# A one-core attention and feed-forward kernel: first loads reordered, first tile transposed in halves, a new TensorE order

## Chip, core and metric

The kernel runs on one core of a Trainium2 chip. The time is device microseconds of one execution; the metric is the median of several. The core has a matrix engine (TensorE, PE in the profile; PEld is its weight load), VectorE (DVE), ScalarE (ACT), GpSimd (POOL) and SyncE (SP). SyncE and ScalarE issue the loads, stores and DMA transposes here. Matmuls accumulate in PSUM, eight banks of 512 float32 columns in each of 128 partitions; everything else lies in SBUF.

## What is computed

A layer norm, then the sum of three things: x itself, a linear attention with softmax feature maps (16 heads of 28), and a feed-forward block with silu. Sizes: 2048 tokens, width 448, feed-forward width 1792, all bfloat16.

```python
def _A_ref(x, wqkv, w_phi, wo):
    qkv = (x @ wqkv).reshape(B, S, 3, H, Dh)  # then transposed: q, k, v per head
    pq = einsum("bhsd,hdf->bhsf", q, w_phi); pk = einsum("bhsd,hdf->bhsf", k, w_phi)
    phi_q = concatenate([softmax(pq), softmax(-pq)], -1)
    phi_k = concatenate([softmax(pk), softmax(-pk)], -1)
    kv = einsum("bhsf,bhsd->bhfd", phi_k, v);  z = einsum("bhsf->bhf", phi_k)
    o = einsum("bhqf,bhfd->bhqd", phi_q, kv) / (einsum("bhqf,bhf->bhq", phi_q, z) + 1e-6)
    return o.reshape(B, S, D) @ wo
def _B_ref(x, w1, w2):
    return silu(x @ w1) @ w2

xn = layernorm(A_x)
out = A_x + _A_ref(xn, A_wqkv, A_w_phi, A_wo) + _B_ref(xn, B_w1, B_w2)
```

## The kernel before

The kernel is a small list scheduler and a list of operations. Each operation names its engine, an assumed duration and what it reads and writes; the scheduler puts each engine's operations in an order and places semaphores. Most of TensorE's order is not left to it: `PLAN` is a list of words that was found by a search, and TensorE follows it strictly. A word `aF3@4` is the first half of feed-forward block 3 in banks 4 and 5, `bF3` its second half; `v`, `k`, `q` are projections of two tiles of 128 tokens; `f` folds w_phi into the q and k weights; `K` gathers kv, `U` is attention, `Y` and `F4:3` are parts of the second feed-forward product, `W`, `R`, `r`, `E` the product with wo and the output. The a, b and R words use 64 rows of the array in pairs, the others up to 128.

```python
PLAN = """aF3@4 aF4@0 bF3 aF5@2 av2@6 bF4 bv2 bF5 aF6@0 bF6 av0@4 bv0 aF7@0 aF8@2 aF10@4 bF8 bF10 bF7 f2@26 aF11@4 aF13@0 bF11
bF13 f0@26 aF9@4 aF12@0 bF9 av4@2 ak0@6 bv4 bF12 bk0 ...
... R3,6,13,1,5,10 F11@1:7 F11:6 F11:1 W11 r11"""
```

The loads, in the order of issue. Wp (w_phi) goes out on ScalarE's queue, the rest on SyncE's. `load_w1` loads the rows 0 to 383 of some columns of w1 and, as a second load, the last 128 rows.

```python
load(Wp[:], A_w_phi..., "wphi", eng="act", lat=3000.0)
load_x(0, 1)
load_x(1, 2)
load_x(2, 4)
load_w1(0, 512)
load_w1(512, 1024)
load_x(4, 8)
load_w1(1024, FF)
load_rows4(wv_sb, A_wqkv, 2 * D, 3 * D, "wv")
load_x(8, 12)
load_x(12, 16)
...   # w2 and wo, behind the transposes
```

Layer norm works on tiles of 128 tokens. Tiles 0 to 3 are turned over on TensorE into PSUM and copied to xnT; tiles 4 to 15 by DMA transposes of two tiles each.

```python
def ln_tile(t):
    ...  # bn_stats, bn_aggr (DVE), sqrt (ACT) and reciprocal (DVE) for t < 4, on POOL for the others
    if t < XN_DMA0:                                    # XN_DMA0 = 4
        norm(xn_sb[:, sl, 0:D], 0, D, 390)
    else:
        norm(xn_sb[:, sl, 0:KF], 0, KF, 370)
        norm(xn_sb[:, sl, KF:512], D - 128, D, 250)
    dstx = xnT[:, t, :, :]
    if t >= XN_DMA0:
        if t % 2:
            dma_t(xnT[:, t - 1:t + 1, ...], xn_sb[:, sl - 1:sl + 1, :], 1300.0, f"xnT_dma{t}", 1350.0)
        return
    tps = bank16[4 + t % 2][:, 0:512]...
    transposes([(tps[:, kt, :], xn_sb[:, sl, KS[kt]:KS[kt] + 128]) for kt in range(4)], f"tr{t}")
    if t < 3: act(dstx, tps, ACTF.Identity, 512, f"ev{t}")
    else:     copy(dstx, tps, 512, f"ev{t}")
```

The head of TensorE's work, ahead of the plan: feed-forward blocks 0, 1 and 2 (columns 0 to 255, 256 to 511, 512 to 767 of w1), token tile by token tile, since the tiles come one after another. For each tile and block there are six matmuls of 128 columns.

```python
head = [F(0, 0), F(1, 2), F(2, AUX)]
for t, fs in ((0, head[:2]), (1, head[:2]), (0, head[2:]), (1, head[2:]), (2, head), (3, head)):
    for f in fs:
        f[0](t * 128, t * 128 + 128)
for b, f in zip((0, 2, AUX), head):
    pe_mms(f[1](), "rest", ...)       # the last 64 rows, then
    f[3]()                            # silu on ScalarE
```

The transposes of SyncE have a fixed order. `wT_dma0` to `7` turn over columns of wqkv for the fold (they lie in the memory of Y_sb, where the profile shows them); the fold needs all eight.

```python
chain("wT_dma0 wT_dma1 wT_dma2 wT_dma3 xnT_dma5 wT_dma4 xnT_dma7 wT_dma5 wT_dma6 wT_dma7 xnT_dma9 xnT_dma11 ... w2 wo0 ...".split())
late = next(o.id for o in P.ops if o.name == "rstd15")    # GpSimd's ones come after it
```

At the end each engine's stream is written straight into the program:

```python
for ename, eng in (("sp", nc.sync), ("act", nc.scalar), ("pool", nc.gpsimd), ("dve", nc.vector), ("pe", nc.tensor)):
    emit_engine(ename, eng)
```

Of the kernel before, what the change touches and what calls it, by code (L numbers as in the profile page):

```python
# [140 lines left out]
class _Prog:  # L141
# [68 lines left out]
    def dma(self, fn, xfer, reads=(), writes=(), name="", out_slot=None, eng="sp", issue=480.0, lat=1700.0):  # L210
        o = self.op(eng, issue, fn, reads, writes, name=name)
        o.is_dma = True
        o.xfer = xfer
        o.lat = lat
        o.out_slot = out_slot
        return o

    def schedule(self):
        ops = self.ops
        n = len(ops)  # L220
# [19 lines left out]
        eng_free = {e: 800.0 if e == "sp" else 0.0 for e in ENGINES}  # L240
# [93 lines left out]
PLAN = """aF3@4 aF4@0 bF3 aF5@2 av2@6 bF4 bv2 bF5 aF6@0 bF6 av0@4 bv0 aF7@0 aF8@2 aF10@4 bF8 bF10 bF7 f2@26 aF11@4 aF13@0 bF11  # L334
bF13 f0@26 aF9@4 aF12@0 bF9 av4@2 ak0@6 bv4 bF12 bk0 av6@4 av8@2 ak4@0 bv8 bk4 bv6 av14@6 ak2@2 bv14 bk2 av12@0 ak6@4
bv12 bk6 ak8@6 av10@2 ak10@0 bv10 bk10 bk8 ak12@2 ak14@4 bk12 bk14 aq4@0 Y0@6:3 Y0:2 K0-6 bq4 aq6@4 K6-8 bq6 aq0@2 aq8@0
bq0 bq8 aF15@4 Y0:9 K8-12 bF15 aF19@2 aF14@0 bF19 bF14 aF17@5 s4 aF18@3 bF17 bF18 K12-16 aF16@5 aF21@2 aF24@0 bF21 bF16
bF24 M s6 aF27@2 aF26@4 bF27 aF22@0 bF26 bF22 aF20@6 aq2@2 bF20 aF23@0 aF25@4 bF23 bF25 bq2 U4 s8 F4@1:10 U9@0 s0 aq12@6
aq14@4 aq10@2 s2 bq12 bq10 bq14 F4:3 F4:1 F9@0:10 F8@3:3 F8:3 s10 W4 U8 s12 F8:6 Y1@4:14 F9:4 W9 U2 U0@5 F2@2:6 F2:8
F8:2 U7@6 U12@5 W8 Y3@4:9 Y3:5 W2 s14 W0@5 F7@4:9 F7:1 U1 F7:4 W7 R0,2 R8,7 R4,9 F10@6:5 U6@5 U10 F10:9 U3@3 F5@4:14  # L340
U13@2 F15@51:8 U15 F15:6 F12@2:5 F12:9 U14 F6@0:5 W12 E15 U5 F13@3:11 F6:9 F14@7:5 F13:2 F13:1 U11@1 W5 W3@5 r12 W13
F14:9 W14 r14 W6 W1@2 W10 R3,6,13,1,5,10 F11@1:7 F11:6 F11:1 W11 r11"""


def bass_parallel_sum__linear_kernel_hedgehog__dense_activation_silu__prompt_kernel(
# [12 lines left out]
    KP = 112  # L358
# [17 lines left out]
    with es:  # L376
# [148 lines left out]
        def load(dst, src, name, eng="sp", lat=1700.0):  # L525
            n = 2
            for _, cnt in list(dst.ap):
                n *= cnt
            P.dma(lambda e: e.dma_start(out=dst, in_=src), n / 280.0, writes=[dst], name=name, eng=eng, lat=lat)  # L529

        def load_x(t0, t1):
            load(x_sb[:, t0:t1, :], xt[:, t0:t1, :], f"x{t0}", lat=1400.0)

        def load_rows4(dst, src, c0, c1, name, lat=1700.0):
            load(dst[:, 0:3, :], src[0:KF, c0:c1].rearrange("(k p) f -> p k f", p=128), name, lat=lat)
            load(dst[:, 3, :], src[D - 128:D, c0:c1], name, lat=lat)

        def load_w1(c0, c1, lat=1700.0):
            load_rows4(w1_sb[:, :, c0:c1], B_w1, c0, c1, "w1", lat)

        load(Wp[:], A_w_phi.rearrange("(g hl) d f -> (hl d) g f", g=G), "wphi", eng="act", lat=3000.0)
# [3 lines left out]
        load_w1(0, 512)  # L545
        load_w1(512, 1024)
        load_x(4, 8)
        load_w1(1024, FF)
        load_rows4(wv_sb, A_wqkv, 2 * D, 3 * D, "wv")
        load_x(8, 12)  # L550
        load_x(12, 16)
        load(w2_sb[:], B_w2.rearrange("(f p) d -> p f d", p=128), "w2")
# [4 lines left out]
        def dma_t(dst, src, xfer, name, issue=1235.0, **kw):  # L557
            o = P.dma(lambda e: e.dma_start_transpose(out=dst, in_=src), xfer, lat=650.0, reads=[src] if kw.pop("sbuf", True) else [],
                      writes=[dst], name=name, issue=issue if xfer < 1500.0 else 2000.0, **kw)
            o.crowd = 1  # L560
# [10 lines left out]
        def fold_loads():  # L571
            for a in range(8):
                dma_t(wT_sb[:, a, :], A_wqkv[:, a * KP:a * KP + 128], 600.0, f"wT_dma{a}", (1600.0, 1400.0, 1780.0, 3280.0)[a] if a < 4 else 1300.0, sbuf=False)
# [22 lines left out]
        def ln_tile(t):  # L596
# [16 lines left out]
            def norm(dst, c0, c1, dur):  # L613
                P.op("dve", dur, lambda e: e.tensor_scalar(dst, x_sb[:, t, c0:c1], mv[:, t, 0:1], rstd[:, t:t + 1], ALU.subtract, ALU.mult),  # L614
                     reads=[xs, mv[:, t, 0:1], rstd[:, t:t + 1]], writes=[dst], name=f"xn{t}")

            if t < XN_DMA0:
                norm(xn_sb[:, sl, 0:D], 0, D, 390)
            else:
                norm(xn_sb[:, sl, 0:KF], 0, KF, 370)  # L620
                norm(xn_sb[:, sl, KF:512], D - 128, D, 250)
            dstx = xnT[:, t, :, :]
            if t >= XN_DMA0:
                if t % 2:
                    dma_t(xnT[:, t - 1:t + 1, :, :].rearrange("p i k c -> p (i k) c"),
                          xn_sb[:, sl - 1:sl + 1, :].rearrange("p i c -> p (i c)"), 1300.0, f"xnT_dma{t}", 1350.0)
                return
            tps = bank16[4 + t % 2][:, 0:512].rearrange("p (k c) -> p k c", k=4)
            transposes([(tps[:, kt, :], xn_sb[:, sl, KS[kt]:KS[kt] + 128]) for kt in range(4)], f"tr{t}")
            if t < 3:  # L630
                act(dstx, tps, ACTF.Identity, 512, f"ev{t}")
            else:
                copy(dstx, tps, 512, f"ev{t}")


# [3 lines left out]
        def pair_block(b0, width, lhs, rhs, name):  # L639
            def part(c0, c1):  # L640
                for i in range(2):
                    for n, kt in enumerate((0, 1, 2 + i)):
                        mm(banks[b0 + i][:, c0:c1], lhs(i, kt, slice(0, 128)), rhs(i, kt, slice(0, 128), c0, c1),
                           n == 0 and c0 == 0, False, name)
# [112 lines left out]
        def phi_q(t, pair=False):  # L757
# [8 lines left out]
            if n % 2 or not pair:  # L766
                n0, sp0 = (slot(t) - 1, sp - 1) if pair else (slot(t), sp)
                w = slot(t) - n0 + 1
                dma_t(phT[:, n0:n0 + w, :, :].rearrange("p t c j -> p (t c) j"), phq[:, sp0:sp0 + w, :, :].rearrange("p n c j -> p (n c j)"),
                      1300.0 * w, "phqT")  # L770
# [109 lines left out]
        chain("bnst0 bnag0 bnst1 bnag1 rstd0 xn0 rstd1 xn1 bnst2 bnag2 bnst3 bnag3 rstd2 xn2 rstd3 xn3 ev3".split())  # L880
        chain("ev0 ve2 ev1 ve3 ev2 silu_table".split())
        chain("tr0 tr1 tr2 tr3".split())
# [8 lines left out]
        for t, fs in ((0, head[:2]), (1, head[:2]), (0, head[2:]), (1, head[2:]), (2, head), (3, head)):  # L891
            for f in fs:
                f[0](t * 128, t * 128 + 128)
# [16 lines left out]
        chain("wT_dma0 wT_dma1 wT_dma2 wT_dma3 xnT_dma5 wT_dma4 xnT_dma7 wT_dma5 wT_dma6 wT_dma7 xnT_dma9 xnT_dma11 xnT_dma13 xnT_dma15 w2 "  # L910
              "wo0 wor0 wo1 wor1".split())
        memset(phq[:, :, :, KP:128], 0.0, 400, "phq0")
        late = next(o.id for o in P.ops if o.name == "rstd15")
        ones_column(0, NEK)
        ones_column(NEK, NT)
        for o in P.ops[-2:]:
            o.odeps.add(late)
# [138 lines left out]
        for ename, eng in (("sp", nc.sync), ("act", nc.scalar), ("pool", nc.gpsimd), ("dve", nc.vector), ("pe", nc.tensor)):  # L1056
            emit_engine(ename, eng)
# [28 lines left out]
```

## Time and profile before

| | |
|---|---|
| time, median of 3 | 150.25 us (150.01 to 151.19) |
| span of the profiled execution | 149.0 us |
| TensorE busy | 144.7 us |
| VectorE, ScalarE, GpSimd busy | 91.3, 70.2, 70.9 us |
| first matmul of the head | 6.96 us after the start |
| last sum begins | 146.64 us |

The profile is of one execution. Times are microseconds from the start of the span. A line of the time order has start, duration, engine, source line, operation, what it writes and reads with shapes and how many of them follow each other; in brackets how long the engine had been idle and what ended that. "L468" is the helper that issues all matmuls, so its rows are told apart by what they write and read: hT is the silu output, RA the normalised tile (its memory is later used by phi), phT at the start is w1. SPq and ACTq are the queues of SyncE and ScalarE. TensorE's end times are modelled, so its busy share says that there is a matmul in flight, not that it is at its peak.

### The profile page before, as it was taken

How to read it: one execution, taken by the hardware profiler on the slowest of the kernel's cores; microseconds unless marked ns; L12 is line 12 of the kernel's file. 1: busy time of each engine (PE TensorE's matmuls, PEld its weight loads, DVE VectorE, ACT ScalarE, POOL GpSimd, SP SyncE). 2: the span in 40 equal slices, each digit the busy share in tenths (PEclk: the TensorE clock that was granted, in tenths of full speed). 3: DMA queues.
4: the chain of work that ended last, by engine and by line, in shares of the span. 5: the costliest groups of instructions: out<-in, count | busy, mean ns of one | idle time of the engine just before them, and what ended most of it. 6: DMA issues, size and time to landing. Idle time of an engine off the chain costs nothing.

```text
span 149.0 us, 3394 instructions
## 1 busy us (share of the span) xinstructions
PE 144.7 (97%) x1412; PEld 79.9 (54%) x1412; DVE 91.3 (61%) x186; ACT 70.2 (47%) x86; POOL 70.9 (48%) x82
## 2 busy tenths in 40 slices
PE   7899999999999999999999999999999999999993
PEld 7694434555555565464544445455555567555541
DVE  1859898940198999211995027897552874243354
ACT  3567764557999997975475585910000000000000
POOL 7108568310049999999699900899600000000000
PEclk9999999999999999999999999999999999999999
DMA  5999975999400000000089494078966745240215
GB/s 101 334 372 336 178 134 106 191 243 344 108 0 4 0 4 4 0 4 0 0 94 191 86 186 79 6 139 160 127 139 134 187 116 106 37 101 5 68 68 179
DMA packets 44352, 17.41 MB, mean 117 GB/s; under 512 B 36784, under 2 KB 43952, under 8 KB 44336
## 3 DMA queue, kind: packets, MB, share of 16 engines
q1 hardware_dynamic: 41568, 15.36, 48.5%
q10 hardware_dynamic: 2768, 1.83, 3.8%
q8 instruction: 11, 0.18, 0.5%
q14 instruction: 5, 0.04, 0.1%
HBM read 6.56 MB, written 1.84 MB: 56 GB/s over the span
## 4 chain that ended last, share of the span: by engine, by line
PE 94%; DMA 3%; DVE 1%; SPq 1%; issue 0%; ACT 0%
PE psum L468 93%; DMA x_sb<-in_A_x_dram 3%; SPq L529 1%; DVE st L599 0%; DVE x_sb L842 0%; PE psum L483 0%; ACT ve L603 0%; DVE mv L600 0%
## 5 line engine op out<-in xcount | busy, mean ns | idle before, releaser
L468 PE MATMUL psum<-xnT,phT 64*128 64x512 bf16 (+1 forms) x428 | 45.1, 350 | 0.7 <-ACT ve L603 0.6
L468 PE MATMUL psum<-w_sb,hT 128*128 128x448 bf16 (+1 forms) x238 | 45.4, 342 | 0.0
L488 ACT ACTIVATE hT<-psum 128x1024 bf16<-128x1024 f32 x28 | 27.4, 1024 | 18.0 <-PE psum L468 18.0
L728 DVE TENSOR_REDUCE Rec<-Ek_sb 128x32 f32<-128x896 bf16 (+1 forms) x20 | 24.3, 1247 | 13.7 <-ACT Ek_sb L488 7.9
L468 PEld LDWEIGHTS psum<-xnT,phT 64*128 64x128 bf16 (+1 forms) x428 | 21.1, 95 | 21.3 <-ACT xnT L488 0.9
L468 PEld LDWEIGHTS psum<-w_sb,hT 128*128 128x128 bf16 x238 | 21.6, 98 | 19.0 <-issue 1.5
L763 POOL TENSOR_TENSOR RA<-Ek_sb,Rec 128x896 bf16<-128x896 bf16 x16 | 26.6, 1700 | 9.1 <-ACT Ek_sb L488 7.7
L468 PE MATMUL psum<-Wqk,xnT 64*128 64x432 bf16 x224 | 22.9, 343 | 0.0
L488 ACT ACTIVATE Ek_sb<-psum 128x864 bf16<-128x864 f32 x24 | 20.3, 932 | 2.9 <-issue 2.6
L738 POOL TENSOR_TENSOR Ek_sb<-Ek_sb,Rec 128x896 bf16<-128x896 bf16 x8 | 13.3, 1702 | 11.0 <-DVE Rec L729 11.0
L820 DVE TENSOR_SCALAR den<-psum 128x16 f32<-128x16 f32 x16 | 2.5, 161 | 22.3 <-PE psum L468 22.3
L468 PEld LDWEIGHTS psum<-Wqk,xnT 64*128 64x128 bf16 x224 | 10.6, 94 | 9.5 <-ACT Ek_sb L488 0.2
L738 POOL TENSOR_TENSOR phT<-phT,Rec 128x896 bf16<-128x896 bf16 x8 | 13.3, 1703 | 0.0
L468 PE MATMUL psum<-wv,xnT 64*128 64x448 bf16 x112 | 12.9, 349 | 0.1
L599 DVE BATCH_NORM_STATS2 st<-x_sb 128x6 f32<-128x448 bf16 x16 | 9.7, 605 | 4.2 <-DMA x_sb<-in_A_x_dram 4.1
L614 DVE TENSOR_SCALAR RA<-x_sb,mv,rstd 128x384 bf16<-128x384 bf16 (+2 forms) x28 | 10.6, 417 | 1.3 <-POOL rstd L610 1.2
L468 PE MATMUL psum<-wo_sb,vaug 128*128 128x448 bf16 (+2 forms) x51 | 11.0, 341 | 0.0
L827 DVE TENSOR_TENSOR vaug<-psum,rden 128x448 bf16<-128x448 f32 x16 | 9.9, 624 | 0.4
L842 DVE TENSOR_TENSOR x_sb<-psum,x_sb 128x448 bf16<-128x448 f32 (+2 forms) x14 | 7.6, 585 | 3.8 <-PE psum L468 3.8
L729 DVE RECIPROCAL Rec<-Rec 128x32 f32<-128x32 f32 (+1 forms) x24 | 8.6, 392 | 0.1
L468 PEld LDWEIGHTS psum<-wv,xnT 64*128 64x128 bf16 x112 | 5.4, 94 | 5.6 <-PE psum L468 0.5
L488 ACT ACTIVATE vaug<-psum 128x896 bf16<-128x896 f32 x8 | 7.4, 945 | 1.6 <-PE psum L468 1.6
(49 smaller groups left out, 104.2 us busy)
## 6 DMA issues: line engine op xcount, KB each, us to landing
out_dram<-x_sb ACTq DMA_DIRECT2D x15, 112.0 KB, 1.7
w_sb<-in_B_w_dram SPq DMA_DIRECT2D x1, 1568.0 KB, 7.6
x_sb<-in_A_x_dram SPq DMA_DIRECT2D x3, 448.0 KB, 8.1
phT<-in_B_w_dram SPq DMA_DIRECT2D x2, 384.0 KB, 4.9
wo_sb<-in_A_wo_dram SPq DMA_DIRECT2D x2, 336.0 KB, 7.8
phT<-in_B_w_dram SPq DMA_DIRECT2D x1, 576.0 KB, 7.2
wv<-in_A_wqkv_dram SPq DMA_DIRECT2D x1, 336.0 KB, 7.7
phT<-in_B_w_dram SPq DMA_DIRECT2D x2, 128.0 KB, 4.7
```

The lines of the kernel that those rows point to most:

```text
L468: r = e.matmul(dst, lhsT, rhs, start=st, stop=sp, skip_group_check=True)
L488: P.op("act", d_act(n), lambda e: e.activation(dst, src, func, scale=scale), reads=[src], writes=[dst], table=table, name=name, **keys)
L529: P.dma(lambda e: e.dma_start(out=dst, in_=src), n / 280.0, writes=[dst], name=name, eng=eng, lat=lat)
L599: P.op("dve", 590, lambda e: e.bn_stats(st6[:, t, :], xs), reads=[xs], writes=[st6[:, t, :]], name=f"bnst{t}", okeys_w=["ln"])
L614: P.op("dve", dur, lambda e: e.tensor_scalar(dst, x_sb[:, t, c0:c1], mv[:, t, 0:1], rstd[:, t:t + 1], ALU.subtract, ALU.mult), reads=[xs, ...
L728: P.op("dve", 50 + 967 * n, lambda e: e.tensor_reduce(R2, E4, AXL.X, ALU.add), reads=[E4], writes=[R2], name="Ssum")
L729: P.op("dve", 135 + 210 * n, lambda e: e.reciprocal(R2, R2), reads=[R2], writes=[R2], name="Rrec")
L738: P.op("pool", 1700, lambda e: e.tensor_tensor(E3, E3, Rk[:, :, None].broadcast_to([128, 32, DH]), ALU.mult), reads=[E3, Rk], writes=[E3], ...
L763: P.op("pool", 1700, lambda e: e.tensor_tensor(dst, Eq, Rq.rearrange("p (c j) -> p c j", c=CC)[:, :, :, None].broadcast_to([128, CC, 4, DH ...
L820: P.op("dve", 190, lambda e: e.tensor_scalar(den[:, uq, :], U3[:, :, DH], EPS_DEN, None, ALU.add), reads=[U3[:, :, DH]], writes=[den[:, uq ...
L827: P.op("dve", 620, lambda e: e.tensor_tensor(o3, U3[:, :, 0:DH], rden[:, uq, :, None].broadcast_to([128, H, DH]), ALU.mult), reads=[U3[:, ...
L842: P.op("dve", d_dve(cs.stop - cs.start), lambda e: e.tensor_tensor(res[:, cs], ob, addend[:, cs], ALU.add), reads=[ob, addend[:, cs]], wri ...
```

## The change

It changes the start of the kernel: w1 is loaded in pieces of 256 columns, the first of them by ScalarE, so that the first block has its weights without waiting for a piece twice as large; w_phi, which is needed late, is loaded late. Tile 0 is normalised, transposed and copied in two halves, so that the first matmuls can run on the first 256 features. The matmuls of the head are split accordingly (`steps`). The transposes on SyncE are put in another order. The scheduler's assumed times are corrected, and TensorE's order is searched again with them. GpSimd's ones wait for the last normalise. The streams are written in a block again, not straight.

```diff
-    def dma(..., eng="sp", issue=480.0, lat=1700.0):
+    def dma(..., eng="sp", issue=520.0, lat=1700.0):
-        eng_free = {e: 800.0 if e == "sp" else 0.0 for e in ENGINES}
+        eng_free = {"sp": 800.0, "act": 2550.0, "pe": 0.0, "dve": 0.0, "pool": 0.0}
-PLAN = (as above)
+PLAN = """aF3@4 aF4@0 bF3 bF4 aF6@6 aF5@2 bF6 bF5 av2@4 bv2 av0@6 aF8@2 aF7@0 bF8 aF10@4 bv0 bF10 bF7 f0@26 aF11@4 aF13@0 bF11
+bF13 f2@26 aF9@4 aF12@0 bF9 av4@2 ak0@6 bv4 bF12 bk0 ...
+... R1,13 R10,5 R3,11 F14@5:7 F14:7 W14 r14"""
-        load(Wp[:], A_w_phi..., "wphi", eng="act", lat=3000.0)
         load_x(0, 1)
         load_x(1, 2)
         load_x(2, 4)
-        load_w1(0, 512)
-        load_w1(512, 1024)
+        load_w1(0, 256, "act")
+        load_w1(256, 512)
+        load_w1(512, 768)
         load_x(4, 8)
-        load_w1(1024, FF)
+        load_w1(768, 1280)
+        load_w1(1280, FF)
         load_rows4(wv_sb, A_wqkv, 2 * D, 3 * D, "wv")
         load_x(8, 12)
         load_x(12, 16)
+        load(Wp[:], A_w_phi..., "wphi", lat=2500.0)
...
-                          ..., 1300.0, f"xnT_dma{t}", 1350.0)
+                          ..., 2200.0 if t < 8 else 1600.0, f"xnT_dma{t}", 1350.0)
...
+            if t == 0:
+                norm(xn_sb[:, sl, 0:256], 0, 256, 290, "a")
+                norm(xn_sb[:, sl, 256:D], 256, D, 275)
+                turn_over(0, 2, 4, "0a")        # two transposes into bank 4, a copy of 256 columns
+                turn_over(2, 4, 5, "0")         # the same into bank 5
             else:
+                norm(xn_sb[:, sl, 0:D], 0, D, 390)
+                turn_over(0, 4, (4, 5, 4)[t - 1], str(t))
...
-        chain("... rstd0 xn0 rstd1 xn1 bnst2 ... ev3".split())
-        chain("ev0 ve2 ev1 ve3 ev2 silu_table".split())
-        chain("tr0 tr1 tr2 tr3".split())
+        chain("... rstd0 xn0a xn0 rstd1 xn1 bnst2 ... ev3".split())
+        chain("warm_act w1_0 w1_0r ve0 ve1 ev0a ev0 ve2 ev1 ve3 ev2 silu_table".split())
+        chain("tr0a tr0 tr1 tr2 tr3".split())
-        for t, fs in ((0, head[:2]), (1, head[:2]), (0, head[2:]), (1, head[2:]), (2, head), (3, head)):
-            for f in fs:
+        for f, steps in ((0, (0, 1)), (1, (0, 1)), (0, (2,)), (1, (2,)), (2, (0, 1, 2))):
+            head[f][0](0, 128, steps)
+        for t in range(1, 4):
+            for f in head:
                 f[0](t * 128, t * 128 + 128)
-        chain("wT_dma0 wT_dma1 wT_dma2 wT_dma3 xnT_dma5 wT_dma4 xnT_dma7 wT_dma5 wT_dma6 wT_dma7 xnT_dma9 ...".split())
+        chain("x8 wT_dma0 wT_dma1 wT_dma2 xnT_dma5 x12 wphi xnT_dma7 wT_dma3 wT_dma4 wT_dma5 wT_dma6 wT_dma7 xnT_dma9 ...".split())
-        late = next(o.id for o in P.ops if o.name == "rstd15")
+        late = max(o.id for o in P.ops if o.name == "xn15")
...
-        for ename, eng in (("sp", nc.sync), ("act", nc.scalar), ...):
-            emit_engine(ename, eng)
+        with nc.Block() as block:
+            @block.tensor
+            def _(pe):
+                emit_engine("pe", pe)
+            ...   # the same for scalar, vector, gpsimd and sync
```

## The prediction

> **What bounds the kernel now.** I read five views of the kernel before, in this order. First, the engine totals and the slices of the page.
>
> ```profile
> PE 144.7 (97%) x1412; PEld 79.9 (54%) x1412; DVE 91.3 (61%) x186; ACT 70.2 (47%) x86; POOL 70.9 (48%) x82
> ...
> PE   7899999999999999999999999999999999999993
> ```
>
> TensorE (PE) is busy in every slice, and only the first two and the last are below nine tenths. Then the chain that ended last, in order of time:
>
> ```profile
> 1.73 4.04 DMA x_sb<-in_A_x_dram
> ...
> 6.98 1.17 PE psum L468 x18
> ...
> 20.82 125.80 PE psum L468 x1204
> ...
> 146.64 0.62 DVE x_sb L842
> ```
>
> From 6.98 us on the chain is TensorE's queue. Only the first 7 us and the last 2.4 us (the last sum, its store) belong to anything else, so a change can gain in two ways: start the real matmuls earlier and keep them fed, or take pauses out of the row. The chain's first link is the load of tiles 2 and 3 of x (issued 1.73, landed 4.04 us later, at 5.77). Third, the start in order of time:
>
> ```profile
> 3.11 0.63 DVE L599 BATCH_NORM_STATS2 st<-x_sb 128x6 f32<-128x448 bf16 x1 [3.11 <-DMA x_sb<-in_A_x_dram]
> ...
> 5.93 0.60 ACT L488 ACTIVATE xnT<-psum 128x512 bf16<-128x512 bf16 x1 [0.92 <-PE psum L483]
> ...
> 6.96 1.19 PE L468 MATMUL psum<-xnT,phT 128*128 128x128 bf16 x18 [0.63 <-ACT ve L603]
> ```
>
> Statistics begin when tile 0 lands (3.11); its normalise (448 columns, 0.40 us) begins at 4.76, its four transposes at 5.30. The first transposed tile is in SBUF at 5.93 + 0.60 = 6.53, but the matmul starts at 6.96. The trace's semaphore events say why: TensorE was waiting for the first piece of w1, whose last part landed at 6.82 (its remainder rows at 7.20; the second 512 columns at 8.30 and 8.63). So two things are tied at the start: a chain x, statistics, normalise, transpose, copy; and a load. Fourth, the DMA issues of the first 14 us:
>
> ```profile
> phT<-in_B_w_dram SPq DMA_DIRECT2D x2, 384.0 KB, 4.9
> ...
> Wp<-in_A_w_phi_dram ACTq DMA_DIRECT2D x1, 24.5 KB, 2.4
> ```
>
> The columns are the number of loads, the size of each and the median time from issue to landing. Up to 13.5 us the loads are a stream of some 370 GB/s, so what is asked for first lands first. The tiny Wp load is in it, too: 448 packets of 56 bytes between 2.0 and 3.0 us, and behind them the first 32 packets of x tiles 2 and 3 took over 0.3 us each, where the same size later took 0.075. Fifth, the transpose queue:
>
> ```profile
> 7.93 7.40 SPq L558 DMA_TRANSPOSE Y_sb<-in_A_wqkv_dram  x4
> 15.37 1.31 SPq L558 DMA_TRANSPOSE xnT<-RA  x1
> ...
> 18.03 1.31 SPq L558 DMA_TRANSPOSE xnT<-RA  x1
> 19.38 3.88 SPq L558 DMA_TRANSPOSE Y_sb<-in_A_wqkv_dram  x3
> ```
>
> SyncE issues one transpose in about 1.3 us and is never free from 7.93 to 29.4. The eighth wqkv transpose (issued 21.99) landed at 25.77; the first fold, which needs all eight, started at 26.28 without waiting. Its slack is about 0.4 us. Just before, xnT of tiles 6 and 7 landed at 21.54 and its first reader started at 21.64: no slack.
>
> **What the skill says.** "DMA: Bandwidth & Descriptors", Issuing engines are not separate DMA queues: loads issued by different engines end up on the same 16 DMA engines and interleave; a second queue saves issue time only. The trace agrees as far as it goes: Wp from ScalarE's queue stands among the packets of x. The same page, Specifications, puts the smallest transfer at full rate at 512 B. Rows of 256 columns of w1 are exactly 512 B; no load here has that size. In this trace 1024-byte packets took 46 ns, 896-byte ones 41 to 45, 256-byte ones about 20, so I estimate 29 ns for 512 B, 283 GB/s over 16 engines. "Advanced Engine Details and Errata", Control Flow Timing: a branch costs about 51 ns. The kernel before has no block to branch to, so no row shows it.
>
> **The change part by part.**
> 1. Wp leaves the front of ScalarE's queue and goes far back in SyncE's. x tiles 0 to 3 lose 448 packets ahead of them. Estimate from the 0.3 us packets: tiles 0 and 1 land 0.1 us sooner, tiles 2 and 3 up to 0.5. The table load of ScalarE (1.25) can start some 0.4 sooner.
> 2. w1 in 256-column pieces. The first (256 KB with its remainder) goes out on ScalarE's queue at about 2.5, the second on SyncE's at 2.2. Before the first reader lies 448 + 256 to 512 KB in place of 448 + 512. I expect the first piece at 5.8 to 6.4 and the third (needed for the third head block) at about 8.0 in place of 8.63.
> 3. Tile 0 in halves. Normalise 0.29 (what the change's own estimate says; a 128-column one takes 0.31 here) in place of 0.40: 0.1 us. Two transposes in place of four before the copy: 2 x 0.106 = 0.2. A copy of 256 columns in place of 512 (0.60 minus 256/1.2 ns = 0.39): 0.2. First matmul at 6.96 - 0.43 (the wait for w1) - 0.5 = about 6.1.
> 4. But that 0.85 us doesn't survive. With x tiles 2 and 3 come a chain of its own: statistics on VectorE 5.79, copy of tile 2 at 8.41 to 9.01, then 36 matmuls of 0.056 us = 2.0 us for tiles 2 and 3. VectorE can't begin tile 2 much sooner: the two half normalises take 0.57 in place of 0.40, so it is free at about 5.85, less the 0.1 of part 1. The head then ends at 9.0 + 0.06 + 2.0 = 11.05 in place of 11.54: **-0.5**.
> 5. The order. I counted, in both orders, turns between 64-row and 128-row work on TensorE: 19 and 19 (each costs 0.10 us extra in the trace). Blocks whose second half directly follows their first: two before (F6, v0), one after (v2); the pauses there were 0.23 us each: **-0.2**. Number of matmuls, banks of the last tile, last words (a whole F, W, r) are alike, so the tail of 2.4 us stays.
> 6. Transpose queue: three wqkv transposes before xnT of tiles 4 and 5 in place of four; then x tiles 12 to 15 and Wp, then xnT of 6 and 7, and five wqkv. SyncE has one load more before its first transpose (15 in place of 14, 0.5 us), so starts at 8.4; three transposes at 1.3 to 1.7 bring it to 12.8 to 13.3; xnT, two loads, xnT take it to 16.3 to 17.0, and the eighth wqkv transpose is issued at 22.0 to 22.8. With the 3.8 us it took to land, the fold can start at 25.8 to 26.6. TensorE, 0.7 us ahead, is there at about 25.5. It waits 0.3 to 1.1 us: **+0.4**, my choice from the lower half, since the stall of the fourth transpose before (2.45 us) goes with the shorter backlog.
> 7. Streams back in a block: branches at the start, a joining of engines at the end. No row; the joining of engines at the start of this trace, which is of the same kind, fits in 0.2 to 0.4 us. **+0.3**, an estimate from that.
> 8. Waiting for the last normalise in place of the last reciprocal root before GpSimd's ones, and wider assumed transfer times: order only, nothing on the path.
>
> Sum: -0.5 - 0.2 + 0.4 + 0.3 = 0.0. Since the new order was searched with longer assumed transfers for transposes, I lean 0.3 to the good side: **149.95 us**.
>
> **Rivals.**
> - *The fold gives it all back.* For it: 0.4 us of slack, SyncE never free, one load more ahead. Against: the stall of the fourth transpose may vanish, and the queue then runs 1 us ahead. It would give 150.3 to 150.8.
> - *The start is all gain.* If x tiles 2 and 3 land at 5.2 and the fold's transposes come in time, 0.9 us from the head and 0.2 from the row: 149.2, with the block's price 149.5. For it: the slow packets behind Wp. Against: VectorE's own chain.
> - *Small packets.* Six loads of 512-byte rows (768 KB with remainders) cost 0.6 us of bandwidth by my estimate; w1 from column 768, needed at about 11.1, then lands at 11.0 to 11.5 and TensorE stops before the fourth block. Gives 150.2.
> - *The block costs more than I think* (instructions fetched anew after the branch): 150.5 to 151.
>
> **Range and chances.** All terms are parts of a microsecond against 150.25, whose own runs lie 1.2 us apart. The rivals span 149.2 to 150.9, which is my range. 2% is 3.0 us, beyond the sum of all terms: 0.02 faster, 0.97 within, 0.01 slower.
>
> **What would show it.** Part 3: first matmul at about 6.1, after a copy of 128x256. Part 4: a pause between the matmuls of tile 0 and tile 1 or 2, and the first silu of hT at about 11.5 in place of 11.98. Part 5: one pause of TensorE on itself in place of two. Part 6: the BDphi matmuls, and whether TensorE waits before them. Part 7: the first load's issue time against 0.80, and the time from the last sum to the end of the span. I am wrong if the long row of TensorE no longer runs without a break after the folds, or if the tail grows by over 0.5 us.

## The result, and the profile after

| | before | after |
|---|---|---|
| time, median of 6 runs each | 150.22 us (150.01 to 151.19) | 152.34 us (151.97 to 152.78) |
| span of the profiled execution | 149.0 us | 150.6 us |
| first silu of hT | 11.98 | 13.48 |
| first fold (BDphi matmuls) begins | 26.28 | 27.48 |
| last sum begins | 146.64 | 147.86 |
| last sum to the end of the span | 2.35 us | 2.74 us |
| time of the profiled execution less its span | 1.26 us | 1.73 us |

The changed kernel is slower: ratio 1.013, 95% interval 1.0098 to 1.0162. The prediction was 149.95 us, with 150.9 at the upper end of its range. (All ratios here leave disturbed executions out, so they need not equal the ratio of two medians.)

The table already divides the loss between the two profiled executions (the fold's matmuls are those that read BDphi). First fold and last sum, before and then after:

```profile
26.28 0.96 PE L468 MATMUL psum<-BDphi,Y_sb 112*128 112x112 bf16 x16
146.64 0.62 DVE L842 TENSOR_TENSOR x_sb<-psum,x_sb 128x448 bf16<-128x448 f32 x1 [0.22 <-PE psum L468]
```

```profile
27.48 0.71 PE L468 MATMUL psum<-BDphi,Y_sb 112*128 112x112 bf16 x11
147.86 0.62 DVE L850 TENSOR_TENSOR x_sb<-psum,x_sb 128x448 bf16<-128x448 f32 x1 [0.60 <-PE psum L468]
```

From the first fold to the last sum both kernels take the same time: 146.64 - 26.28 = 120.36 us before, 147.86 - 27.48 = 120.38 after. So 120 us of a newly searched order gained nothing, and the difference comes from two places: the fold begins 1.20 us later, and what follows the last sum is longer by 0.39 us within the span and 0.47 behind it. 1.20 + 0.02 + 0.39 + 0.47 = 2.08 us, the difference of the two profiled executions (152.33 and 150.25). Before's six runs here were on the good side: in the later series its median is 150.59 to 151.43 us, and the loss of the unchanged after, measured again there, is a ratio of 1.0121.

The engine totals and slices of the page after: TensorE looks as full as before.

```profile
PE 145.9 (97%) x1412; PEld 81.0 (54%) x1412; DVE 89.9 (60%) x187; ACT 70.4 (47%) x87; POOL 71.0 (47%) x82
...
PE   7899999999999999999999999999999999999992
...
PEclk9999999999999999999999999999999999999999
```

The chain that ended last, after:

```profile
1.28 2.97 DMA x_sb<-in_A_x_dram
4.24 0.02 issue
4.27 0.64 DVE st L601
...
7.21 1.92 PE psum L468 x18
...
20.76 127.07 PE psum L468 x1218
...
147.86 0.62 DVE x_sb L850
```

Its first load is now x tile 1, not tiles 2 and 3, and the statistics at 4.27 are those of tile 1. The start in order of time, after, shows why they stand in the way:

```profile
0.80 1.28 ACT L488 ACT_TABLE_LOAD   x1 [0.80 <-PEq L1099]
1.04 0.98 ACTq L529 DMA_DIRECT2D phT<-in_B_w_dram  x2
...
4.27 0.63 DVE L601 BATCH_NORM_STATS2 st<-x_sb 128x6 f32<-128x448 bf16 x1 [0.30 <-DMA x_sb<-in_A_x_dram]
...
5.19 0.59 DVE L616 TENSOR_SCALAR RA<-x_sb,mv,rstd 128x256 bf16<-128x256 bf16 x2
...
6.09 0.66 ACT L488 ACTIVATE xnT<-psum 128x256 bf16<-128x256 bf16 x2 [0.66 <-PE psum L483]
...
6.20 0.62 DVE L601 BATCH_NORM_STATS2 st<-x_sb 128x6 f32<-128x448 bf16 x1
...
7.00 2.12 PE L468 MATMUL psum<-xnT,phT 128*128 128x128 bf16 x18
```

ScalarE issues the first piece of w1 at 1.04, during its table load and not after it, between SyncE's loads of tiles 0 and 1. That piece lands early (3.96, its remainder at 5.08), but tile 1 lands at 4.24 in place of 3.49. VectorE's order puts tile 1's statistics ahead of tile 0's normalise, which begins at 5.19 in place of 4.76. The 18 matmuls take 2.12 us where they took 1.19: 0.107 us each in place of 0.056, up to 10.16. The granted-clock row (PEclk) shows nines all the same, because this trace holds no clock record before 10.11; the spacing of matmuls tells.

The last part of w1 lands at 11.81 us (before 12.39), so w1 does not arrive later than it did.

SyncE's queue in order of time, after:

```profile
7.72 0.71 SPq L529 DMA_DIRECT2D x_sb<-in_A_x_dram  x1
8.47 3.97 SPq L560 DMA_TRANSPOSE Y_sb<-in_A_wqkv_dram  x3
14.48 1.26 SPq L560 DMA_TRANSPOSE xnT<-RA  x1
15.78 0.58 SPq L529 DMA_DIRECT2D x_sb<-in_A_x_dram  x1
16.41 0.44 SPq L529 DMA_DIRECT2D Wp<-in_A_w_phi_dram  x1
16.89 1.26 SPq L560 DMA_TRANSPOSE xnT<-RA  x1
18.19 6.92 SPq L560 DMA_TRANSPOSE Y_sb<-in_A_wqkv_dram  x5
```

The queue stands empty from 12.44 to 14.48, waiting for the normalise of tile 5 (done at 14.45); before, the fourth wqkv transpose lay there. The last of the five is issued at 23.52 and lands at 26.85, 1.07 us later than before (25.78). In this execution TensorE doesn't wait for it, because the slow matmuls of the head have already made TensorE later still.

### The profile page after: what moved, and what is told of

It is laid out like the page before. It is cut to its first block, busy times and chain, and to the rows that moved or that the text cites. A ratio compares the mean times of both kernels' runs of the same rounds, so it can differ in the third digit from the quotient of the medians.

```text
span 150.6 us, 3415 instructions
## 1 busy us (share of the span) xinstructions
PE 145.9 (97%) x1412; PEld 81.0 (54%) x1412; DVE 89.9 (60%) x187; ACT 70.4 (47%) x87; POOL 71.0 (47%) x82
## 4 chain that ended last, share of the span: by engine, by line
PE 94%; DMA 2%; DVE 1%; issue 0%; SPq 0%; ACT 0%
PE psum L468 93%; DMA x_sb<-in_A_x_dram 2%; PE psum L483 1%; DVE st L601 0%; DVE x_sb L850 0%; SPq L529 0%; ACT xnT L488 0%; DVE RA L616 0%; DVE mv L602 0%; DVE rstd L607 0%
## 5 line engine op out<-in xcount | busy, mean ns | idle before, releaser
L468 PE MATMUL psum<-xnT,phT 64*128 64x512 bf16 (+1 forms) x428 | 46.1, 355 | 0.0
L488 ACT ACTIVATE hT<-psum 128x1024 bf16<-128x1024 f32 x28 | 27.4, 1023 | 15.9 <-PE psum L468 15.9
L468 PEld LDWEIGHTS psum<-xnT,phT 64*128 64x128 bf16 (+1 forms) x428 | 22.2, 97 | 20.2 <-ACT hT L488 0.7
L616 DVE TENSOR_SCALAR RA<-x_sb,mv,rstd 128x384 bf16<-128x384 bf16 (+4 forms) x29 | 9.6, 371 | 1.9 <-POOL rstd L612 1.7
```

What stands on the lines that cost most here:

```text
L468: r = e.matmul(dst, lhsT, rhs, start=st, stop=sp, skip_group_check=True)
L488: P.op("act", d_act(n), lambda e: e.activation(dst, src, func, scale=scale), reads=[src], writes=[dst], table=table, name=name, **keys)
```

## The experiments

Two theories at first. **Rate:** the head ran at the slow matmul rate, a matter of warm-up, and the rest is the block. **Queue:** SyncE's transposes come later, and a fast head would only run into them. The measure that tells them apart is the time from the first silu to the first fold: where nothing waits it is 14.0 to 14.3 us (before 14.30, after 14.00). Waits of TensorE are given here as the profile gives them, as idle time; the expectations count them from the starts of the matmuls, which makes the same wait 0.16 us longer. Each profile is of one execution, and can be the fastest or the slowest of its kernel; the table under experiment 8 says which.

**1. More or fewer warm-up matmuls.** The first kernel is after, the second before.

```diff
-        for i in range(38):     # warm-up matmuls
+        for i in range(44):     # in the second kernel: 32
```

> The changed kernel with 44 warm-up matmuls in place of 38, nothing else. Clock theory: the changed kernel's start leaves TensorE idle for 0.6 and 0.4 us around 5.3 and 6.4, so it stays at the slow rate (0.107 us for a matmul of 128 columns) up to 10.05 us; six more warm-up matmuls fill most of the first pause, the fast rate (0.056) begins before 7 us, the first silu of hT starts at about 11.7 in place of 13.48, and the time is about 150.7 us in place of 152.3. Rival, late loads: the head waits for x and w1, the rate is no matter, and the time stays within 0.3 us of 152.3.

> The kernel before with 32 warm-up matmuls in place of 38, nothing else: a pause of 0.85 us ahead of the first transpose in place of 0.2. Clock theory: the matmuls at 7 us run at 0.107 us until about 10 us, some 29 of them, 29 x 0.051 = 1.5 us lost, 151.6 us in place of 150.2. Rival: the warm-up is of no account for the head, 150.2 us.

With 44, 152.52 us, ratio to before 1.0106 (1.0078 to 1.0134). The head did run at the fast rate (first silu 12.32 in place of 13.48), and nothing came of it: TensorE then stood idle for 1.25 us until 22.35, waiting for xnT of tiles 6 and 7 (the profile names it; landed 22.21), and the fold began at 27.75. So a fast head alone does not mend after's time. With 32, before took 151.03, ratio 0.9966 (0.994 to 0.9992): no loss either, but its profile was at the fast rate from 5.83 on, so the slow head that was to cost 1.5 us did not come about there.

**2. The streams written straight, and the block put into the kernel before.**

```diff
-        with nc.Block() as block: ...          # after, made straight
+        for ename, eng in (("sp", nc.sync), ...): emit_engine(ename, eng)
```

> The changed kernel with the streams written straight in place of the block, nothing else. Block theory: the time from the last sum to the end of the execution shrinks by 0.9 us (0.4 inside the span, 0.5 behind it), so 151.4 us in place of 152.3; the start is unchanged. Rival: the block costs at the start or nothing, and the longer tail is from the stores: 152.3 us or below by less than 0.3.

> The kernel before with the streams in a block, nothing else. Block theory: 0.9 us on top, 151.1 us, all behind the last sum, which stays at 146.6 us of the span. Rival: 150.2 to 150.5 us.

After without the block: 151.48, ratio 1.0025 (1.0001 to 1.0049); in time, then, most of the loss is gone. Before with the block: 151.20, ratio 1.0026 (0.9996 to 1.0057), not to be told from before by time alone. The profiles are clear. Before in a block ends like this, with a span of 149.2 us:

```profile
146.46 0.62 DVE L842 TENSOR_TENSOR x_sb<-psum,x_sb 128x448 bf16<-128x448 f32 x1 [0.23 <-PE psum L468]
```

From there to the end are 2.74 us. Of the 20 profiles of this study the four in a block show 2.74 us, and 1.72 to 1.76 from the end of the span to the time; the straight ones 2.34 to 2.36 and 1.24 to 1.28. The block costs 0.39 + 0.48 = **0.87 us**, all behind the last sum; the first load goes out at 0.80 in both.

Straight, after shows what its own slow head had hidden. This profiled execution, 152.31 us, is the slowest of the kernel's 20, so the waits in it are large ones. TensorE in order of time:

```profile
18.77 2.29 PE L468 MATMUL psum<-wv,xnT 64*128 64x448 bf16 x20
22.21 2.98 PE L468 MATMUL psum<-xnT,phT 64*128 64x512 bf16 x26 [1.15 <-issue]
...
28.36 0.85 PE L468 MATMUL psum<-BDphi,Y_sb 112*128 112x112 bf16 x14 [0.68 <-DMA Y_sb<-in_A_wqkv_dram]
```

Two waits: until 22.21 for xnT of tiles 6 and 7 (landed 22.12; the profile has no name for this wait, the landing and the reader give it one), then for the eighth wqkv transpose (landed 28.22). First silu to fold: 16.07 us.

**3. After once more, unchanged.**

> The changed kernel as it is, once more, beside the three that follow and on the same chip: the measure for how far its single runs lie apart. 152.0 to 152.8 us if the first six runs are typical; if the moment at which TensorE gets its fast rate is a matter of luck, the runs spread over 1.5 us and the median may be 152.3 or a few tenths more.

152.58 us, ratio 1.0121 (1.0056 to 1.0185). In this profile the head was fast from 4.20 on, first silu 12.37, and waits of 0.60 and 0.54 us stood in the same two places; fold at 27.76. With a slow or a fast head, the fold begins at nearly the same time in these two profiles (27.48 and 27.76): whichever of head and queue comes later sets it.

**4. The transpose order: x tiles 12 to 15 behind all transposes, and the first piece of w1 on SyncE.** Both on straight after; the second has both edits. The third puts the new transpose order, with x tiles 12 to 15 and Wp placed as in it, into the kernel before, the fourth is straight after with four wqkv transposes ahead of the first xnT and x tiles 12 to 15 behind the second.

```diff
-chain("x8 wT_dma0 wT_dma1 wT_dma2 xnT_dma5 x12 wphi xnT_dma7 wT_dma3 ... wT_dma7 ...")
+chain("x8 wphi wT_dma0 wT_dma1 wT_dma2 xnT_dma5 xnT_dma7 wT_dma3 ... wT_dma7 x12 ...")        # first, second
+chain("x8 wT_dma0 ... wT_dma3 xnT_dma5 wT_dma4 xnT_dma7 x12 wphi wT_dma5 wT_dma6 wT_dma7 ...")  # fourth
-        load_w1(0, 256, "act")
+        load_w1(0, 256)                                                                        # second
```

> The changed kernel with straight streams (151.48 us), and with the load of x tiles 12 to 15 behind the eighth wqkv transpose and w_phi ahead of the first, so that xnT of tiles 6 and 7 is issued right after that of 4 and 5. Queue theory: these two loads delay xnT of 6 and 7 by 1 us of issue and some data; without them it lands near 20.5 in place of 22.1, the 1.3 us wait of TensorE at 20.7 goes, the fold's own wait stays under 0.3, and the time is 150.2 to 150.5. Rival, rate of TensorE: the queue is no matter, 151.3 to 151.7.

> The same as the second of these four, and the first piece of w1 goes out on SyncE's queue behind x tiles 0 to 3, not on ScalarE's. The piece on ScalarE's queue is issued at 1.04, ahead of x tile 1, which lands at 4.24 in place of 3.5 and holds up the normalise of tile 0. If that is what spoils the early start: x tile 1 lands at 3.5, the first transpose starts at 5.2 in place of 5.7, the first matmul of the head waits for w1 to about 6.2, and 0.3 us are won over the second. If the head is held by w1 all the same: no gain.

> The kernel before with nothing but the changed order of SyncE's transposes and with w_phi and x tiles 12 to 15 loaded between them as in the changed kernel. Queue theory: xnT of tiles 6 and 7 lands about 0.5 to 1 us later than 21.5 and the last wqkv transpose 1 us later than 25.8; TensorE waits for both, 0.8 to 1.2 us on top of the median of before in the same call. Rival: less than 0.3 on top.

> The changed kernel with straight streams (151.48 us) and with SyncE's order as before where it counts: four wqkv transposes, not three, ahead of xnT of tiles 4 and 5, one more between that and xnT of 6 and 7, and x tiles 12 to 15 and w_phi behind both. Queue theory: SyncE no longer stands idle 2 us for tile 5, xnT of 6 and 7 lands by 21.2, the last wqkv transpose by 26.2; TensorE's two waits (1.3 and 0.8 us) shrink below 0.4 together, and the time is 150.0 to 150.5 us. Rival, the first loads themselves or the head are the cause: 151.2 to 151.7.

The first: both waits gone (fold at 26.15), and yet 154.35, ratio 1.0249 (1.0188 to 1.031). The x tiles landed at 28.4, and their normalise and the folded weights behind it on VectorE came late:

```profile
34.71 0.74 PE L468 MATMUL psum<-wv,xnT 64*128 64x448 bf16 x6 [1.28 <-DVE Wqk L594]
36.19 1.10 PE L468 MATMUL psum<-Wqk,xnT 64*128 64x432 bf16 x6 [0.73 <-DVE Wqk L594]
```

The two waits are only half of the 4.1 us by which fold to last sum grew (124.47 in place of 120.36). Right behind them the clock was halved for 3.41 us, and 20 matmuls ran in a stretch that holds 40 in before (the last three columns are granted clock, DMA share and GB/s):

```profile
36.40:39.81 3.41, 3.41 (x20) 1.62 (x18) 0.00 (x0) 0.92 (x1) 1.77 (x2) 0.50 0.94 208
```

The second: 154.46, ratio 1.0259. Tile 1 landed at 3.90 and the first matmul began at 6.42, but the first silu at 12.23, so the 0.3 us were not won. It has 18 loads ahead of the first transpose (issued 10.56), and its fold waited until 27.84. The third, before with the new transpose order: 150.98, ratio 1.0006 (0.9978 to 1.0033), not the loss of 0.8 to 1.2 that I expected, though its profile shows the fold waiting 0.73 us and its lowest run is 150.50 against 149.95. The fourth: 151.66, ratio 1.0052 (1.0027 to 1.0077); both waits gone and fold at 26.12 in its profile (its fastest execution), but the second fold waits 0.55 us until 30.76, behind VectorE's work on the late x tiles. The expectation was missed again: in these orders the shortage moves to another reader.

**5. Filler matmuls between the transposes and the head, to hold the rate.** On the kernel before; on the fourth kernel of experiment 4; and on before with after's TensorE order.

```diff
+        for i in range(7): matmul(banks[3][:, 0:128], ones_bf, ones_bf)   # after tr1, with 40 warm-ups
+        (4, after tr0, with 43 warm-ups, in the second kernel)
```

> The kernel before with its pauses ahead of the first real matmul filled: 40 warm-up matmuls in place of 38, and seven more between the transposes of tile 1 and the first matmul. Rate theory: the single runs of before lie between 149.9 and 152.2 because the fast rate starts, by luck, before 7 us or only near 10; with the pauses filled nearly all runs have it by 7.6: median 150.1 to 150.5, three quarters of the runs below 150.8, where before has a median near 151.3. Rival: the spread has another cause (slow DMA engines, for one), and median and spread stay.

> The first of these four with 43 warm-up matmuls and four more behind the transposes of tile 0. If the rate is what is left: 0.2 to 0.5 us below the first, and less spread. If not: the same, or 0.1 us more for the matmuls added.

> The second of these four with the newly searched order of TensorE and nothing else of the change. Order theory: one pause of TensorE on itself less (0.23 us) and equal turns between 64 and 128 rows: 0.1 to 0.3 us below the second. Rival: the new order was searched for another head and queue, and waits in this one: 0.3 us or more above.

Before with fillers: 150.56, ratio 0.9966 (0.9942 to 0.9989). The second: 151.84, ratio 1.0062, with waits of 0.74 and 1.05 us: no gain. Its head had the fast rate from 3.80 on, so here too the rate was not what was left. The third: 151.25, ratio 1.0024 (1.0001 to 1.0046), 0.69 above the first in the same series. One line of its TensorE says why:

```profile
21.30 2.98 PE L468 MATMUL psum<-xnT,phT 64*128 64x512 bf16 x26 [0.55 <-issue]
```

The new order is ready for tokens 512 to 1023 (block 8) at 20.75, where the old one first reads them at 21.64; xnT of tiles 6 and 7 lands at 21.20.

**6. What remains without the block, part by part.** All straight: after with the old TensorE order; after with the old transpose order; after with both, so that only the new head is left.

```diff
-PLAN = (as after)                                  # first and third kernel
+PLAN = (as before)
-chain("x8 wT_dma0 wT_dma1 wT_dma2 xnT_dma5 x12 wphi xnT_dma7 ...")        # second and third
+chain("x8 x12 wphi wT_dma0 wT_dma1 wT_dma2 wT_dma3 xnT_dma5 wT_dma4 xnT_dma7 ...")
```

> The kernel after with straight streams, but with the TensorE order of the kernel before. If the new order's early demand for the tokens of tiles 4 to 7 is a cost, the wait of 1.31 us at xnT of tiles 6 and 7 is gone or below 0.3, the wait for the fold (0.8) stays, and the time is 150.8 to 151.3, 0.2 to 0.6 below the 151.48 of the straight form. If the order is innocent (only the queue matters), 151.4 to 151.8, since the two clash pauses come back.

> The kernel after with straight streams and its new TensorE order, but with four wqkv transposes ahead of the first xnT, as before (x tiles 12 to 15 and w_phi are loaded ahead of all of them). If the queue's idle time in front of the first xnT is the cost, the fold does not wait, a wait of 0.4 to 0.9 us at xnT of tiles 6 and 7 stays because the new order asks for it early, and the time is 151.0 to 151.4. If the queue's order is innocent, 151.5 as the straight form.

> Only the new first loads and the first tile in halves; the TensorE order, the transpose order and the straight streams are those of the kernel before. If the new head gains what it was meant to (0.5 us), 150.5 to 150.8, below the kernel before, and first silu of hT at 11.5. If it gains nothing because x tile 1 and the first tile's normalise come later, as the traces so far say: first silu at 12.1 to 12.4 and a time within 0.3 us of the kernel before.

151.84 (ratio 1.0075, 1.0049 to 1.0101), 152.82 (1.0115, 1.0066 to 1.0163) and 152.16 (1.0085, 1.0042 to 1.0127). The first: the xnT wait is gone as expected, the fold's wait stays (0.73) and the time doesn't fall: the eighth transpose lands at 27.29 and the fold begins at 27.53, so TensorE's earlier saving is lost there. The second: worse, not better; TensorE waits 2.00 us for xnT. The third was the surprise: a head without any new order loses 1.3 us, and TensorE waits 0.93 us until 23.18 for xnT of tiles 6 and 7 (landed 23.09). SyncE's queue in it:

```profile
7.92 1.16 SPq L529 DMA_DIRECT2D x_sb<-in_A_x_dram  x2
9.12 0.72 SPq L529 DMA_DIRECT2D Wp<-in_A_w_phi_dram  x1
9.88 7.40 SPq L560 DMA_TRANSPOSE Y_sb<-in_A_wqkv_dram  x4
17.32 1.31 SPq L560 DMA_TRANSPOSE xnT<-RA  x1
18.67 1.26 SPq L560 DMA_TRANSPOSE Y_sb<-in_A_wqkv_dram  x1
19.98 1.31 SPq L560 DMA_TRANSPOSE xnT<-RA  x1
```

The first transpose is issued at 9.88 (before 7.93), xnT of tiles 6 and 7 at 19.98 (18.03). Seventeen loads lie ahead of it in place of fourteen: w1 in eight on SyncE where there were six, and Wp. That made a new theory: **the number of loads on SyncE**.

**7. The new head with fourteen loads, and the kernel before with seventeen.**

```diff
-        load_w1(512, 768); load_x(4, 8); load_w1(768, 1280); load_w1(1280, FF)   # head alone
+        load_w1(512, 1024); load_x(4, 8); load_w1(1024, FF)                      # and wphi on ScalarE behind w1
-        load_w1(0, 512)                                                          # before
+        load_w1(0, 256); load_w1(256, 512)                                       # and wphi on SyncE behind x12
```

> The new head with as many loads on SyncE's queue as the kernel before (14 in place of 17): w1 in pieces of 256, 256, 512 and 768 columns, the first on ScalarE, w_phi on ScalarE behind it; TensorE order and transpose order as before. If the three more loads on SyncE (about 0.5 us each, first transpose issued at 9.88 in place of 7.93) are what cost the head-only form its 1.3 us: first transpose issued at 7.7 to 8.2, the eighth of wqkv at 21.8 to 22.3, waits at xnT of tiles 6 and 7 below 0.2, time 150.4 to 151.2, within 0.4 us of the kernel before. If the new head itself is the cost (x tile 1 later, first tile later): 151.6 to 152.2, as the head-only form.

> The kernel before with three more loads on SyncE's queue and nothing else: the first piece of w1 in two (256 columns each) and w_phi behind the x tiles in place of on ScalarE. If the number of loads ahead of the transposes sets the time: first transpose issued at 9.4 to 9.9, xnT of tiles 6 and 7 issued at 19.5 to 20.0, TensorE waits 0.9 to 1.4 us for it, time 1.0 to 1.6 us above the kernel before. If the queue has room for them: within 0.3 us of the kernel before, or below it, since x tiles 2 and 3 land sooner without w_phi's small packets.

The first: 151.70, ratio 1.0015 (0.9984 to 1.0046): no longer to be told from before. In its profile (its fastest execution, 150.41 us, while that of the head alone was its median) the queue is back, and TensorE doesn't wait:

```profile
8.00 7.14 SPq L559 DMA_TRANSPOSE Y_sb<-in_A_wqkv_dram  x4
15.18 1.31 SPq L559 DMA_TRANSPOSE xnT<-RA  x1
16.53 1.27 SPq L559 DMA_TRANSPOSE Y_sb<-in_A_wqkv_dram  x1
17.84 1.31 SPq L559 DMA_TRANSPOSE xnT<-RA  x1
```

The second: 152.63 against 151.03, ratio 1.0092 (1.0067 to 1.0117), as the theory asked. The first transpose is issued at 10.48, and its queue is that of the head-only kernel to 0.1 us from the first xnT on, and TensorE:

```profile
20.47 1.73 PE L468 MATMUL psum<-wv,xnT 64*128 64x448 bf16 x14
23.55 4.71 PE L468 MATMUL psum<-xnT,phT 64*128 64x512 bf16 x42 [1.35 <-issue]
```

So three more loads on SyncE, put into a kernel that is otherwise that of before, cost as much as the whole head. In both kernels the number of loads changed together with the width of w1's pieces and the place of Wp, so that the number alone is the cause is not shown. Why the transposes come two us late is only half settled. Issue is one part: 7.93 to 9.88. The stream itself is another, by the stretches 6 to 8 and 8 to 10 us (last two columns: DMA share, GB/s) of the head with 17 loads, then with 14:

```profile
6.00:8.00 2.00, 1.34 (x20) 1.02 (x18) 1.88 (x7) 1.42 (x5) 0.00 (x0) 1.00 0.93 273
8.00:10.00 2.00, 1.93 (x34) 1.87 (x35) 1.45 (x5) 1.34 (x4) 0.00 (x0) 1.00 0.95 292
```

```profile
6.00:8.00 2.00, 1.27 (x21) 1.10 (x21) 1.90 (x7) 1.50 (x5) 0.94 (x1) 1.00 1.06 386
8.00:10.00 2.00, 2.00 (x38) 1.94 (x36) 1.47 (x5) 1.34 (x3) 0.00 (x0) 1.00 1.04 384
```

About 100 GB/s less for 4 us is 0.4 MB, one us of stream; x tiles 12 to 15 land at 16.93 and 15.87. The kernel before shows the same: 380 and 372 GB/s, with three more loads 311 and 310. Packet size is the smaller part, at least from 8 to 10 us: there the 17-load head moves mostly packets of 1024 bytes, the other 1536, and by their median times (46 and 65 ns over 16 engines) that is 356 against 378 GB/s, while 292 and 384 were moved. The rest, a lower busy share and single packets that took longer, is not explained.

**8. A version from all this.** Before with the fillers of experiment 5, no block, its own loads, xnT of tiles 6 and 7 ahead of the fifth wqkv transpose, and an order without a second half directly behind its first.

```diff
-PLAN = """... aF6@0 bF6 av0@4 bv0 aF7@0 aF8@2 aF10@4 bF8 ...
+PLAN = """... aF6@0 av0@4 bF6 bv0 aF8@2 aF7@0 aF10@4 bF8 ...
-chain("... xnT_dma5 wT_dma4 xnT_dma7 wT_dma5 ...")
+chain("... xnT_dma5 xnT_dma7 wT_dma4 wT_dma5 ...")
```

> The kernel before with 40 warm-up and 7 filler matmuls, xnT of tiles 6 and 7 ahead of the fifth wqkv transpose, and the two places where a block's second half directly follows its first taken out of the order. If both small pauses of 0.225 us were on the path: 0.1 to 0.4 us below the 150.56 of the form with fillers alone, so about 150.3. If xnT or the fold takes their place as a wait: 150.5 to 151.

150.08 us against 150.59 in the same series, ratio 0.995 (0.9929 to 0.997), faster than both kernels; against the fillers alone (0.9966, 0.9942 to 0.9989) a gain is not shown. The order asks for block 8 early, as the new one does, and the tokens are there:

```profile
20.29 0.92 PE L468 MATMUL psum<-wv,xnT 64*128 64x448 bf16 x8
21.05 4.75 PE L468 MATMUL psum<-xnT,phT 64*128 64x512 bf16 x42
26.09 0.95 PE L468 MATMUL psum<-BDphi,Y_sb 112*128 112x112 bf16 x16 [0.29 <-ACT hT L488]
```

Both small pauses are gone, but 0.29 us of the gain is lost again in front of the fold, which now waits for a silu (ACT hT).

The queue of the kernels that matter, in one table (us; loads are those on SyncE ahead of the first transpose; "landed" is xnT of tiles 6 and 7, then the eighth wqkv transpose; the last column has the time of the profiled execution, then the lowest and the median of the kernel):

| kernel | loads | first transpose issued | landed | first silu to fold | profiled; lowest, median |
|---|---|---|---|---|---|
| before | 14 | 7.93 | 21.55, 25.78 | 14.30 | 150.25; 150.01, 150.22 |
| after, straight | 15 | 9.21 | 22.12, 28.22 | 16.07 | 152.31; 150.79, 151.48 |
| old TensorE order | 15 | 8.82 | 21.01, 27.29 | 15.03 | 151.48; 150.91, 151.84 |
| old transpose order | 17 | 10.49 | 23.08, 27.56 | 16.18 | 152.54; 151.92, 152.82 |
| head alone | 17 | 9.88 | 23.09, 27.95 | 15.72 | 152.16; 151.48, 152.16 |
| head, 14 loads | 14 | 8.00 | 21.38, 25.47 | 14.24 | 150.41; 150.41, 151.70 |
| before, 17 loads | 17 | 10.48 | 23.46, 27.76 | 15.77 | 152.14; 151.74, 152.63 |

## Why the prediction was wrong

Two steps failed. Part 7 booked 0.3 us for the block, which cost 0.87. Parts 3 to 6 had head, order and queue bring the fold 0.3 us forward on balance; it came 1.20 us later. The sum missed by 2.39 us. By its own terms: the block 0.57 too small; head, order and queue together +1.20 at the fold in place of -0.3, so 1.5; and the lean of 0.3 to the good side. That is 2.37.

This is the account of two profiled executions. By whole series the shares differ: without the block, after is only 0.25% above before (0.4 us), and with it 1.2 to 1.3%, so there the block is the largest miss. Nor do the parts add up: the head alone costs 0.85%, the new order of TensorE 0.24% (0.6% above the same kernel with the old order), the new transpose order 0.06%, and all of them together without the block 0.25%. Why they cost less together stays open.

- **Part 1** held in small: tiles 2 and 3 landed at 5.45 in place of 5.77. But tile 1 landed 0.75 later. Part 2's first piece, issued at 1.04 and not at 2.5, fits as the cause: with that piece on SyncE's queue tile 1 landed at 3.90 (experiment 4) and 3.38 (before with 17 loads). The reading of the packets was rough: of the first 32 packets of tiles 2 and 3, nine took over 0.3 us, which is their mean.
- **Part 2** got the weights right and more: first piece at 5.08, not 5.8 to 6.4; w1 no longer holds the head. (Its stream of 370 GB/s was 268 from 3 to 6 us and 386 from 6 to 13.5.) Its true price was not in the sum at all: two more loads of w1 on SyncE, with Wp three. Part 6 booked "one load more, 0.5 us", since the new transpose order moves x tiles 12 to 15 and Wp behind an xnT; experiment 7 shows what three cost in before, 1.4 us (0.92% of 151). After itself has fifteen loads ahead, and what its one more costs was not measured.
- **Parts 3 and 4**: first matmul 6.69 to 6.81 in the fast-head profiles of after, not 6.1, and the first silu 12.29 to 12.37 in place of 11.5. The step that failed is "VectorE free at about 5.85": it begins tile 2's statistics at 6.20, before at 5.79, for it had waited for tile 1 first. That is +0.3 to +0.4 for the head in place of -0.5. The pause after tile 0 came as predicted (0.25 idle at 7.9 in straight after). In after's own profile the slow rate added another 1.1.
- **Part 5** was right in count, one pause in place of two (14.00 us from silu to fold in place of 14.30). It overlooked that the same order asks for xnT of tiles 6 and 7 about 0.9 us earlier (20.75 against 21.64), which I had myself found to have no slack: 0.55 us of idle in experiment 5, and 0.69 in its time.
- **Part 6** failed in size, and is the main step on the way to the fold: I took the lower half of 0.3 to 1.1. The eighth transpose was issued at 23.52 in after, 25.56 straight, 24.85 in the repeat, not at 22.0 to 22.8. I let xnT of tiles 4 and 5 follow the three transposes at once. In after SyncE waited for tile 5's normalise instead (2.0 us of empty queue), and the fourth transpose that had filled that time stood at the far end; that the stall of 2.45 us would go was no gain, since it had lain in that same hole. In straight after no such hole is left: there the stalls did not go, but moved to the third transpose (2.22 us of issue), to xnT of tiles 4 and 5 (2.43) and to the seventh (2.30), where about 1.3 is usual.
- **Part 7**: mechanism right, mis-sized, and entirely at the end. The joining at the start was the wrong thing to size it by, and a price behind the span (0.48) can't be read from a span.
- **Part 8** as said, nothing seen.

Of the rivals, "the fold gives it all back" was right and too mild. "The block costs more than I think" was right as well; the reason it gave, instructions fetched anew, was not tested. "Small packets" named a real slowing of the stream but the wrong victim: w1 landed in time, the transposes behind it did not. The packets of 512 bytes took 27 ns (median, after), close to the 29 estimated.

The Trainium skill, "DMA: Bandwidth & Descriptors", Issuing engines are not separate DMA queues, says of a second issuing engine that it saves only the time to initiate the DMA, "which is usually small relative to the DMA itself". Here that time counted: about 0.5 us a load on the queue that the transposes share. "TensorE: Matmul & The Clock Gate", What's actually happening, says that the window which sets TensorE's rate is free-running and not reset by a kernel, so that the turn to the full rate varies, by 500 ns either way; the two profiles of unchanged after agree that it moves, but show 6 us (10.16 and 4.20), and the measurement stands. Whether the warm-ups explain before's spread (149.94 to 154.2 in 71 runs) stays open: 32 warm-ups and 40 with fillers gave the same 0.9966.

## What to carry to other kernels

Count instructions on each issuing queue up to its last urgent one: splitting a load to start earlier can delay everything behind it on that queue, and a bound that shows only some 15 us later can take the gain back. When one reader waits for two feeds in turn, taking away the earlier wait may only lengthen the later one; look at the landing of the last thing needed. Before reading a wait off a profile, see where that execution stands among the runs of its kernel. Before trusting a search over an order, ask at what time the new order first asks for each tile, against when it lands.

## What the runs showed that I had not expected

- The row from the first fold to the last sum takes 120.34 to 120.38 us in 16 of the 20 profiles, under both orders. The other four are experiments that delayed x tiles 12 to 15.
- A block's price is 0.87 us and lies wholly behind the last sum, over half of it behind the profiled span.
- Why after's first head was slow and its repeat's was not can be read from TensorE's own idle time. In the 15 profiles with clock records, the unbroken full-clock stretches that start in the head last 139.95, 143.36 or 146.77 us, steps of 3.41 (one, in the first kernel of experiment 4, ends after 30.72 us). In the 3.41 us before full clock began, TensorE was busy for 82% or more in all of them, in the 3.41 us before that for 78% or less: 78% in after (3.28 to 6.70), where before had 92% in its last stretch (3.19 to 6.60). The half clock of experiment 4 followed a stretch that was 41% busy. Where between 78 and 82% the line lies, no run shows.
- ScalarE's queue issued a load at 1.04 us, inside a table load that ran from 0.80 to 2.08.
- The issue of a DMA transpose, 1.26 to 1.3 us when undisturbed, was stretched up to 3.2 us while the x loads ahead of it were still landing (head with 14 loads, fourth transpose, issued 11.91; tiles 12 to 15 landed 15.87), at no cost to TensorE.
